# Summing the last four rows of an output projection in two PSUM banks

## The chip, the core and the metric

The kernel runs on one core of a Trainium2 chip. The metric is the device time of one execution in microseconds (us), as the median of several runs. A profile of one execution is read beside it. Engines are named as the profile names them: PE (TensorE, matmuls; PEld are its weight loads), DVE (VectorE), ACT (ScalarE), POOL (GpSimd), SP (SyncE). A q behind an engine's name means its queue, which issues transfers (DMA) and waits for semaphores.

## What is computed

One decode step for one token of width 1024: a layer norm, then an attention over the last 4096 positions of a cache (32 query heads, 4 key and value heads of width 128) with its output projection `wo`, and in parallel an MLP; both are added to the input.

```
xn = layernorm(x)
q  = (xn @ wq) as 32 heads of 128;  k, v = last 4096 rows of each cache, 8 heads share one
o  = softmax(q k^T / sqrt(128)) v
A  = o.reshape(1, 4096) @ wo
B  = gelu(layernorm(xn) @ w1 + b1) @ w2 + b2
out = x + A + B                       # 1 x 1024, bf16
```

Weights and caches are bf16, some 40 MB in all, each read once.

## The kernel before

The kernel streams weights and caches through a ring of four large buffers in SBUF, filled by transfers on the SP queue in a fixed order: keys, `wq`, `w1`, values, `w2`, `wo`. A transfer into a buffer waits for the last reader of what was there. Everything else follows the arrival of the data.

Products of one row vector with a weight matrix are done as matmuls with one column of stationary weights (`lhsT`, 128 x 1) and 512 columns of the matrix streaming past. Each gives one row of 512 sums. To use more of the PE array, the results of two halves of a row (or four quarters) are put at partitions 0, 32 and so on, by `tile_position`.

The part that the change touches is the last one. The final sum of 1024 columns is kept in one PSUM bank, the tile `accf` (128 x 512 fp32): partition 0 holds columns 0 to 511, partition 32 columns 512 to 1023. It starts from `x + b2` (line 178). Then a loop over `chunk_src` (line 337) adds 28 chunks of `w2`, each weighted by a column of `hT` (the MLP's hidden values), and 32 chunks of `wo`, each weighted by a column of `o8` (the attention output, copied from the PSUM tile `o8_ps` at line 332). A chunk is 128 x 1024, that is one row of 1024 for each partition; the text calls a chunk of `wo` a row of it. Each takes two matmuls, one a half (line 341), with `start=False`, so that they add up in `accf`.

The second 16 rows of `wo` arrive in five transfers of 8, 4, 2, 1 and 1 rows, each with a semaphore of its own, so that PE can start on what is there. The very last row is cut into columns 0 to 319 and 320 to 511 (`N1 = 320`), so four matmuls. At the end DVE copies 320 columns of `accf` to the bf16 tile `res` (line 345) and ACT the other 192 (line 346). Two transfers, one on the SP queue and one on the ACT queue, write the two halves of the result (lines 348 and 349).

PSUM tiles that live shortly come from the pool `ps_f`, two banks that are used in turn: `sp`, `mT_ps`, `mc_ps`, `rs_ps`, `o_all` and `o8_ps` among them. Waits between engines are put in by the framework from which tile each operation reads and writes; two engines that read one PSUM tile are put in order. The order of instructions on each engine is that of the program text.

Of the kernel before, what the change touches and what calls it, by code (L numbers as in the profile page):

```python
# [8 lines left out]
FP32 = mybir.dt.float32  # L9
BF16 = mybir.dt.bfloat16  # L10
ACT = mybir.ActivationFunctionType
ALU = mybir.AluOpType
# [4 lines left out]
def kernel(  # L17
# [14 lines left out]
    nc = tc.nc  # L32
    P = 128
# [20 lines left out]
    consts = ctx.enter_context(tc.tile_pool(name="consts", bufs=1))  # L54
# [4 lines left out]
    ps_f = ctx.enter_context(tc.tile_pool(name="ps_f", bufs=2, space=bass.MemoryType.PSUM))  # L59
# [3 lines left out]
    def ring_tile(name):  # L63
        return ring.tile([P, RING_ELEMS], BF16, tag="ring", name=name, align_bytes=256)
# [13 lines left out]
    for i in range(2):  # L78
        t = ring_tile(f"wq{i}")
# [8 lines left out]
    ident_f = consts.tile([P, P], FP32)  # L88
# [83 lines left out]
    accf = ps_acc.tile([P, 512], FP32, tag="accf")  # L172
# [3 lines left out]
    for half in range(2):  # L176
        pr = 32 * half
        nc.tensor.matmul(accf[pr:pr + 1, :], lhsT=ones_bf[0:2, 0:1], rhs=xb2[:, 512 * half:512 * half + 512],
                         start=True, stop=False, tile_position=(0, pr))
# [24 lines left out]
    for i in range(2):  # L204
        t = ring_tile(f"w1{i}")
# [9 lines left out]
    chunk_src = []  # L215
    w2_v = B_w2.rearrange("(p c) n -> p c n", p=P)
    for i in range(2):
        nr = CW2 // 2
        t = ring_tile(f"w2{i}")
# [4 lines left out]
    for i, cuts in enumerate([[0, 16], [0, 8, 12, 14, 15, 16]]):  # L224
        nr = CWO // 2
        t = ring_tile(f"wo{i}")
# [6 lines left out]
    for i, w3 in enumerate(wq_tiles):  # L233
        for r in range(4):
            c = 4 * i + r
            for j in range(NJQ):
                b, t = divmod(j, 4)
                nc.tensor.matmul(accq[32 * t:32 * t + 1, b, :], lhsT=xnT[:, c:c + 1], rhs=w3[:, r, j * 512:(j + 1) * 512],  # L238
                                 start=(c == 0), stop=(c == C - 1), tile_position=(0, 32 * t))
# [8 lines left out]
    for j in range(8):  # L248
        t, b = divmod(j, 2)
        nc.tensor.matmul(acch[32 * t:32 * t + 1, b, :NH], lhsT=ones_bf[0:1, 0:1], rhs=b1_row[:, j * NH:(j + 1) * NH],  # L250
                         start=True, stop=False, tile_position=(0, 32 * t))
    for i, w3 in enumerate(w1_tiles):
        for r in range(4):
            c = 4 * i + r
            for b in range(2):
                for t in range(4):
                    j = 2 * t + b
                    nc.tensor.matmul(acch[32 * t:32 * t + 1, b, :NH], lhsT=yT[:, c:c + 1], rhs=w3[:, r, j * NH:(j + 1) * NH],  # L258
                                     start=False, stop=(c == C - 1), tile_position=(0, 32 * t))
# [3 lines left out]
    for g in range(Hkv):  # L263
        b, th = divmod(g, 2)
# [6 lines left out]
    for a in range(WQ4 // 512):  # L271
        sp = ps_f.tile([P, 512], FP32, tag="pf", name="sp")
        for R in range(4):
            for g in range(Hkv):
                c0 = WQ4 * R + 512 * a
                nc.tensor.matmul(sp[32 * R:32 * R + 32, :], lhsT=qm[:, g, :], rhs=kT[:, g, c0:c0 + 512],  # L276
                                 start=(g == 0), stop=(g == Hkv - 1), tile_position=(0, 32 * R))
# [41 lines left out]
    for c in range(NCH):  # L319
        nc.tensor.matmul(o_all[:].rearrange("h g d -> h (g d)"), lhsT=eTb[:, 32 * c:32 * c + 32], rhs=v4[:, :, c, :],  # L320
                         start=(c == 0), stop=(c == NCH - 1))
# [12 lines left out]

    vec = {"h": lambda c: hT[:, c, 0:1], "o": lambda c: o8[:, c:c + 1]}
    N1 = 320
    for idx, (kind, c, wap) in enumerate(chunk_src):
        last = idx == len(chunk_src) - 1
        for n0, n1 in ((0, N1), (N1, 512)) if last else ((0, 512),):
            for half in range(2):  # L340
                nc.tensor.matmul(accf[32 * half:32 * half + 1, n0:n1], lhsT=vec[kind](c),  # L341
                                 rhs=wap[:, half * 512 + n0:half * 512 + n1],
                                 start=False, stop=last and n0 > 0, tile_position=(0, 32 * half))
    res = consts.tile([33, 512], BF16)
    nc.vector.tensor_copy(out=res[:, 0:N1], in_=accf[0:33, 0:N1])  # L345
    nc.scalar.copy(out=res[:, N1:512], in_=accf[0:33, N1:512])  # L346
    out_v = out.rearrange("a b (t n) -> (a b t) n", t=2)
    nc.sync.dma_start(out=out_v[0:1, :], in_=res[0:1, :])
    nc.scalar.dma_start(out=out_v[1:2, :], in_=res[32:33, :])
# [30 lines left out]
```

## Time and profile before

| | us |
|---|---|
| median of 3 runs | 102.22 (102.12 to 102.40) |
| the profiled execution | 102.17 |
| its span, first to last instruction | 100.4 |
| busy in it: PE / DVE / ACT | 49.5 / 48.8 / 33.8 |
| transfers | 39.92 MB, mean 398 GB/s |

The profile lists, for each group of equal instructions, source line, engine, operation, output and inputs with their shapes, count, busy time, mean duration in ns, and the idle time of the engine just ahead of them with what ended it. The chain of waits follows the last instruction back through whatever released it. A granted clock (PEclk) of 1.00 is full speed of PE. Durations of matmuls are modelled from their starts, so the records of neighbours overlap. Of the span, 1.8 us are missing to the execution's own time; they lie outside.

```profile
PE   0165200009400930194865718997390980299970
DMA  2999999999999998999999998999999999999910
```

These two rows of the page are the busy tenths of PE and of the transfers in 40 slices of the span: the transfers are busy from the first slice almost to the last, and PE works in bursts.

### The profile page before, as it was taken

What the parts mean: (1) busy time and instruction counts of PE and PEld (TensorE: products, weight loads), DVE (VectorE), ACT (ScalarE), POOL (GpSimd) and SP (SyncE); (2) the same over time, 40 slices, a digit from 0 to 9 for tenths busy, and PEclk for the clock granted to TensorE, in tenths of its full rate; (3) what the DMA queues carried; (4) which work ended last, traced back from release to release, by engine and by line L of the source; (5) the groups of instructions that cost most, each with busy time, mean ns of one, the idle gap of its engine ahead of it and who ended that gap; (6) DMA issues with size and microseconds to landing.
All of it is one profiled execution on the core that took longest, in us unless ns stands there. A gap on an engine that the chain in (4) does not pass through costs nothing.

```text
span 100.4 us, 944 instructions
## 1 busy us (share of the span) xinstructions
PE 49.5 (49%) x355; PEld 19.5 (19%) x355; DVE 48.8 (49%) x89; ACT 33.8 (34%) x36; POOL 3.8 (4%) x16
## 2 busy tenths in 40 slices
PE   0165200009400930194865718997390980299970
PEld 0131200003100300022522203343130320033310
DVE  5445499999999999995136061502600000000010
ACT  5000004999999999942020148000000000000001
POOL 6006200000000000000000000000000000000000
PEclk9999999999999999999998555599999669556997
DMA  2999999999999998999999998999999999999910
GB/s 29 396 438 424 558 431 444 418 418 418 418 418 403 514 384 369 491 411 400 393 434 428 424 506 377 498 400 423 457 411 415 431 457 405 418 418 408 380 42 1
DMA packets 2878, 39.92 MB, mean 398 GB/s; under 512 B 309, under 2 KB 311, under 8 KB 698
## 3 DMA queue, kind: packets, MB, share of 16 engines
q1 hardware_dynamic: 2866, 39.85, 93.3%
q8 instruction: 3, 0.05, 0.2%
q10 hardware_dynamic: 8, 0.01, 0.0%
q14 instruction: 1, 0.01, 0.0%
HBM read 39.86 MB, written 0.00 MB: 397 GB/s over the span
## 4 chain that ended last, share of the span: by engine, by line
DMA 80%; PE 13%; SPq 2%; issue 1%; DVE 0%; ACT 0%
DMA wq<-in_A_wq_dram 27%; DMA wo<-in_A_wo_dram 25%; DMA v_sb<-in_A_v_cache_dram 23%; PE o_all L320 9%; DMA k_sb<-in_A_k_cache_dram 5%; PE accq L238 4%; SPq L229 2%; SPq L213 1%; DVE res L345 0%; PE accf L341 0%; ACT res L346 0%
## 5 line engine op out<-in xcount | busy, mean ns | idle before, releaser
L200 ACT COPY kT<-kt_scr 32x1024 bf16<-32x1024 bf16 x26 | 27.1, 1042 | 14.5 <-DVE kt_scr L186 14.2
L186 DVE STREAM_TRANSPOSE kt_scr<-k_sb 128x4096 bf16<-128x4096 bf16 x4 | 17.4, 4412 | 0.0
L202 DVE COPY kT<-kt_scr 32x1024 bf16<-32x1024 bf16 x38 | 15.9, 419 | 0.5
L238 PE MATMUL accq<-wq,xnT 128*1 128x512 bf16 x64 | 7.2, 626 | 18.2 <-DMA wq<-in_A_wq_dram 18.2
L345 DVE CAST res<-accf 33x320 bf16<-33x320 f32 x1 | 0.5, 483 | 25.2 <-PE accf L341 25.2
L341 PE MATMUL accf<-wo,o 128*1 128x512 bf16 (+2 forms) x66 | 9.9, 460 | 5.0 <-DMA wo<-in_A_wo_dram 5.0
L346 ACT CAST res<-accf 33x192 bf16<-33x192 f32 x1 | 0.3, 313 | 35.5 <-DVE res L345 35.5
L320 PE MATMUL o_all<-v_sb,eTb 128*32 128x512 bf16 x32 | 9.2, 459 | 1.6 <-DMA v_sb<-in_A_v_cache_dram 1.6
L341 PE MATMUL accf<-w,hT 128*1 128x512 bf16 x56 | 8.1, 452 | 2.5 <-DMA w<-in_B_w_dram 2.5
L258 PE MATMUL acch<-w,yT 128*1 128x448 bf16 x64 | 5.7, 525 | 6.2 <-DMA w<-in_B_w_dram 6.2
L238 PEld LDWEIGHTS <-xnT 128*1 128x1 bf16 x64 | 2.1, 116 | 22.5 <-issue 22.5
L341 PEld LDWEIGHTS <-o 128*1 128x1 bf16 x66 | 3.3, 98 | 11.9 <-issue 9.8
L320 PEld LDWEIGHTS <-eTb 128*32 128x32 bf16 x32 | 3.5, 113 | 6.9 <-issue 3.0
L341 PEld LDWEIGHTS <-hT 128*1 128x1 bf16 x56 | 2.7, 96 | 7.2 <-issue 5.0
L258 PEld LDWEIGHTS <-yT 128*1 128x1 bf16 x64 | 1.9, 107 | 9.5 <-issue 9.0
L276 PE MATMUL sp<-kT,qm 128*32 128x512 bf16 x32 | 3.4, 588 | 0.4 <-DVE qm L267 0.4
L323 DVE TENSOR_TENSOR o_m<-o_all,grs 32x512 f32<-32x512 f32 x1 | 0.7, 679 | 5.6 <-PE o_all L320 5.6
L123 PE MATMUL x_ps<-ones_bf,xb 1*128 1x1 bf16 x8 | 0.6, 198 | 4.7 <-DMA xb<-in_A_x_dram 4.7
L315 DVE STREAM_TRANSPOSE hT<-h_sb 128x896 bf16<-128x896 bf16 x1 | 1.7, 1704 | 2.4 <-ACT h_sb L313 2.4
L298 ACT ACTIVATE e<-sc,nmx 128x1024 bf16<-128x1024 f32 x1 | 1.1, 1147 | 4.9 <-DVE nmx L295 4.9
L276 PEld LDWEIGHTS <-qm 128*32 128x32 bf16 x32 | 2.1, 133 | 1.4 <-issue 0.9
L281 ACT COPY sc<-sp 128x512 f32<-128x512 f32 x1 | 0.6, 586 | 4.5 <-PE sp L276 4.5
(81 smaller groups left out, 32.0 us busy)
## 6 DMA issues: line engine op xcount, KB each, us to landing
w<-in_B_w_dram SPq DMA_DIRECT2D x4, 3584.0 KB
wq<-in_A_wq_dram SPq DMA_DIRECT2D x2, 4096.0 KB, 26.7
k_sb<-in_A_k_cache_dram SPq DMA_DIRECT2D x4, 1024.0 KB, 6.8
wo<-in_A_wo_dram SPq DMA_DIRECT2D x1, 4096.0 KB, 30.7
v_sb<-in_A_v_cache_dram SPq DMA_DIRECT2D x1, 2048.0 KB, 19.5
v_sb<-in_A_v_cache_dram SPq DMA_DIRECT2D x2, 1024.0 KB, 23.4
wo<-in_A_wo_dram SPq DMA_DIRECT2D x1, 2048.0 KB
wo<-in_A_wo_dram SPq DMA_DIRECT2D x1, 1024.0 KB
```

Source lines behind the costliest of these rows:

```text
L186: nc.vector.transpose(out=scr[:, g, :], in_=k2[:, g, :])
L200: nc.scalar.copy(out=dst, in_=src)
L202: nc.vector.tensor_copy(out=dst, in_=src)
L213: nc.sync.dma_start(out=v4[:, g0:g1, :, :], in_=src)
L229: nc.sync.dma_start(out=tv[:, a:b, :], in_=wo_v[:, nr * i + a:nr * i + b, :])
L238: nc.tensor.matmul(accq[32 * t:32 * t + 1, b, :], lhsT=xnT[:, c:c + 1], rhs=w3[:, r, j * 512:(j + 1) * 512], start=(c == 0), stop=(c == C ...
L258: nc.tensor.matmul(acch[32 * t:32 * t + 1, b, :NH], lhsT=yT[:, c:c + 1], rhs=w3[:, r, j * NH:(j + 1) * NH], start=False, stop=(c == C - 1) ...
L276: nc.tensor.matmul(sp[32 * R:32 * R + 32, :], lhsT=qm[:, g, :], rhs=kT[:, g, c0:c0 + 512], start=(g == 0), stop=(g == Hkv - 1), tile_posit ...
L298: nc.scalar.activation(out=e128[:], in_=sc[:], func=ACT.Exp, bias=nmx[:], scale=scale, accum_out=l_loc[:])
L315: nc.vector.transpose(out=hT[:], in_=h_sb[:].rearrange("p (d c) -> p c d", c=CW2))
L320: nc.tensor.matmul(o_all[:].rearrange("h g d -> h (g d)"), lhsT=eTb[:, 32 * c:32 * c + 32], rhs=v4[:, :, c, :], start=(c == 0), stop=(c == ...
L341: nc.tensor.matmul(accf[32 * half:32 * half + 1, n0:n1], lhsT=vec[kind](c), rhs=wap[:, half * 512 + n0:half * 512 + n1], start=False, stop ...
```

## The change

The last four rows of `wo` no longer go into `accf`. The loop over the first 56 chunks is as before (both halves, 512 columns) and closes `accf`. ACT then copies columns 320 to 511 of it to an fp32 tile in SBUF (`bulk1`) and DVE columns 0 to 319 (`bulk0`). Two new PSUM tiles of the pool `ps_f`, `acct0` (320 columns) and `acct1` (192 columns), are zeroed by DVE in the 33 partitions that are read later. The last four rows are summed into them, each row cut at 320 as only the last was before. Ahead of the third of the four, two fp32 matmuls with columns of the identity `ident_f` add `bulk1` to `acct1`, one a half. At the end DVE adds `acct0` and `bulk0` into `res`, and ACT copies `acct1` into `res`.

In the program's order of instructions, the first memset stands on DVE ahead of the copy of `o8` and the second behind it; the fp32 matmuls wait for ACT's copy of the bulk; DVE's copy of the bulk waits for ACT's; the two output transfers wait for DVE and ACT both. The weight loads ahead of the fp32 matmuls are part of these instructions. Nothing changes on the SP queue ahead of the output.

```diff
-    for idx, (kind, c, wap) in enumerate(chunk_src):
-        last = idx == len(chunk_src) - 1
-        for n0, n1 in ((0, N1), (N1, 512)) if last else ((0, 512),):
+    TAIL = 4
+    n_bulk = len(chunk_src) - TAIL
+    for idx, (kind, c, wap) in enumerate(chunk_src[:n_bulk]):
+        for half in range(2):
+            nc.tensor.matmul(accf[32 * half:32 * half + 1, :], lhsT=vec[kind](c), rhs=wap[:, half * 512:(half + 1) * 512],
+                             start=False, stop=(idx == n_bulk - 1), tile_position=(0, 32 * half))
+    cols = ((0, N1), (N1, 512))
+    bulk = [consts.tile([33, b - a], FP32, name=f"bulk{i}") for i, (a, b) in enumerate(cols)]
+    nc.scalar.copy(out=bulk[1][:], in_=accf[0:33, N1:512])
+    nc.vector.tensor_copy(out=bulk[0][:], in_=accf[0:33, 0:N1])
+    acct = [ps_f.tile([P, b - a], FP32, tag="pf", name=f"acct{i}") for i, (a, b) in enumerate(cols)]
+    for t in acct:
+        nc.vector.memset(t[0:33, :], 0.0)
+    for idx, (kind, c, wap) in enumerate(chunk_src[n_bulk:]):
+        if idx == TAIL - 2:
             for half in range(2):
-                nc.tensor.matmul(accf[32 * half:32 * half + 1, n0:n1], lhsT=vec[kind](c),
+                nc.tensor.matmul(acct[1][32 * half:32 * half + 1, :], lhsT=ident_f[0:33, 32 * half:32 * half + 1], rhs=bulk[1][:],
+                                 start=False, stop=False, tile_position=(0, 32 * half))
+        for t, (n0, n1) in zip(acct, cols):
+            for half in range(2):
+                nc.tensor.matmul(t[32 * half:32 * half + 1, :], lhsT=vec[kind](c),
                                  rhs=wap[:, half * 512 + n0:half * 512 + n1],
-                                 start=False, stop=last and n0 > 0, tile_position=(0, 32 * half))
+                                 start=(idx == 0), stop=(idx == TAIL - 1), tile_position=(0, 32 * half))
     res = consts.tile([33, 512], BF16)
-    nc.vector.tensor_copy(out=res[:, 0:N1], in_=accf[0:33, 0:N1])
-    nc.scalar.copy(out=res[:, N1:512], in_=accf[0:33, N1:512])
+    nc.vector.tensor_tensor(out=res[:, 0:N1], in0=acct[0][0:33, :], in1=bulk[0][:], op=ALU.add)
+    nc.scalar.copy(out=res[:, N1:512], in_=acct[1][0:33, :])
```

In the changed kernel the fp32 matmuls are at line 353, the matmuls of the last four rows at 357, DVE's sum at 361 and ACT's copy at 362.

## The prediction

> **What bounds the kernel now.** I read the chain of waits first, because only what lies on its last link can move the time, then the timeline of the last microseconds, then the groups for the price of each operation.
>
> The page says that the span is one long transfer; the chain in order of time shows how the last transfer turns into the end.
>
> ```profile
> span 100.4 us, 944 instructions
> DMA 80%; PE 13%; SPq 2%; issue 1%; DVE 0%; ACT 0%
> ...
> 71.55 25.41 DMA wo<-in_A_wo_dram
> 96.96 0.04 issue
> 97.00 0.40 PE accf L341 x4
> 97.40 0.02 issue
> 97.42 0.49 DVE res L345
> 97.92 0.02 issue
> 97.94 0.31 ACT res L346
> ```
>
> The transfers carry 80% of the chain, and the change touches none of them. What it can touch is the stretch behind the landing of the last `wo` row at 96.96: the matmuls of that row, then DVE's copy of 320 columns, then ACT's copy of 192, one after the other, then the two output transfers. The timeline of that stretch has each step's start and length, and in brackets what its engine waited for:
>
> ```profile
> 95.52 1.25 PE L341 MATMUL accf<-wo,o 128*1 128x512 bf16 x8
> 95.79 0.30 PEld L341 LDWEIGHTS <-o 128*1 128x1 bf16 x4 [0.18 <-issue]
> 96.39 0.08 PEld L341 LDWEIGHTS <-o 128*1 128x1 bf16 x2 [0.30 <-issue]
> 97.00 0.38 PE L341 MATMUL accf<-wo,o 128*1 128x320 bf16 x4 [0.23 <-DMA wo<-in_A_wo_dram]
> 97.42 0.48 DVE L345 CAST res<-accf 33x320 bf16<-33x320 f32 x1 [25.17 <-PE accf L341]
> 97.94 0.31 ACT L346 CAST res<-accf 33x192 bf16<-33x192 f32 x1 [35.49 <-DVE res L345]
> 98.28 0.32 SPq L348 DMA_DIRECT2D out_dram<-res  x1
> ```
>
> I number the last 16 rows of `wo` 0 to 15. The eight matmuls from 95.52 are rows 11 to 14, two halves each; the weight loads at 95.79 and 96.39 mark where rows 12 and 14 began, with idle time ahead of them, so PE is waiting for data there and no longer working off a backlog. Row 15 starts at 97.00. ACT's copy waits for DVE's, not for PE: that serial 0.31 us is what the change goes after. From row 15's start to the output transfer is 98.28 - 97.00 = 1.28 us.
>
> **The change part by part.** *The finish.* Row 15 now goes into two PSUM tiles, and DVE and ACT each read one. In the changed program ACT's last copy waits for PE and for the second memset, not for DVE's sum, so the two run side by side. DVE no longer waits for the 192-column pair either. The prices:
>
> ```profile
> L341 PE MATMUL accf<-wo,o 128*1 128x320 bf16 x2 | 0.3, 296 | 0.2 <-DMA wo<-in_A_wo_dram 0.2
> L341 PE MATMUL accf<-wo,o 128*1 128x192 bf16 x2 | 0.2, 244 | 0.0
> L323 DVE TENSOR_TENSOR o_m<-o_all,grs 32x512 f32<-32x512 f32 x1 | 0.7, 679 | 5.6 <-PE o_all L320 5.6
> L241 DVE CAST q_sb<-accq 128x512 bf16<-128x512 f32 x1 | 0.7, 692 | 0.0
> L320 PEldq EVENT_SEMAPHORE  x1: 51/51/51, 60.4 to 60.4; - x1
> ```
>
> At 512 columns a two-input DVE operation out of PSUM (679 ns) costs what a copy does (692), so I price the new sum of 320 columns like the old copy, 0.48 us. Let T be the start of row 15. DVE starts at T + 0.30 (its pair) + 0.04 (the step from 97.38, the last matmul's end, to 97.42), and ends at T + 0.82. ACT starts 0.08 us later than DVE (the 52 ns by which 320 and 192 columns differ say 0.41 ns a column, so a 192-column pair streams for 0.08) and needs 0.31: it ends at T + 0.73, earlier. The transfers were issued 0.03 us after the last copy (97.94 + 0.31 to 98.28). Now they wait for two engines; the second wait is a semaphore instruction of its own, for which I take 0.05 us (the 51 ns row; the lower bound is nothing). The issue comes at T + 0.82 + 0.03 + 0.05 = T + 0.90 in place of T + 1.28. **Gain if T stays at 97.00: 0.38 us.**
>
> *The bulk copies and the fp32 matmuls.* These lie in front of rows 14 and 15 on PE, so they decide T. Row 11's second half is the last of the bulk. It starts at 95.52 and lasts 0.38:
>
> ```profile
> L341 PE MATMUL accf<-wo,o x66: 243/379/634, 87.3 to 97.1; 128*1 128x512 bf16 x62, 128*1 128x320 bf16 x2, 128*1 128x192 bf16 x2
> L242 ACT CAST q_sb<-accq 128x512 bf16<-128x512 f32 x1 | 0.6, 587 | 2.8 <-DVE q_sb L241 2.8
> L281 ACT COPY sc<-sp 128x512 f32<-128x512 f32 x1 | 0.6, 586 | 4.5 <-PE sp L276 4.5
> ```
>
> An fp32 result costs ACT no more than a bf16 one (586 against 587), so its copy of 192 columns is 0.31: 95.90 + 0.04 + 0.31 = 96.25, and with the step to PE 96.30. Meanwhile PE works off rows 12 and 13, which take 0.22 us each whether cut at 320 or not, from 95.79 to 96.22; it then waits 0.08 us for ACT. Nothing but rows 14 and 15 is queued behind that wait, and behind them the two finishing operations and the output transfers. DVE's copy of the bulk runs after ACT's, 96.29 to 96.77, and is covered by DVE's own wait until T + 0.34.
>
> An fp32 matmul of this shape is not in the trace. The nearest rows:
>
> ```profile
> L286 PE MATMUL mT_ps<-ident_f,m_loc 128*1 128x128 f32 x1 | 0.3, 269 | 2.1 <-DVE m_loc L284 2.1
> L302 PE MATMUL rs_ps<-l_loc,sel x2: 193/203/213, 58.6 to 58.7; 128*32 128x1 f32 x2
> 53.77 0.27 PE L286 MATMUL mT_ps<-ident_f,m_loc 128*1 128x128 f32 x1 [2.07 <-DVE m_loc L284]
> 53.98 0.36 PE L258 MATMUL acch<-w,yT 128*1 128x448 bf16 x4
> ```
>
> In bf16 a matmul lasts 165 ns plus 0.41 ns a column (296 and 244). The fp32 one of 128 columns lasts 269, so 104 for its columns: 0.81 ns each, twice bf16. One fp32 product is recorded as two passes (`rs_ps`, x2 for one call), so 192 columns cost 2 x 0.156 = 0.31 us a half. The two halves lie in different column strips of the array. If they overlap as the bf16 halves do, both take 0.31; if the second can start only with the first one's second pass, 0.47; if they queue, 0.62; if every pass ran to the end of its record (4 x (0.165 + 0.156)), 1.28. The `rs_ps` passes began within 0.1 us of each other with records of 0.2, which speaks against the last; I take **0.47**. Coming back to full rows costs something too: from `mT_ps` to the next matmul are 0.21 us, 0.10 more than its columns. So F = 0.47 + 0.10 = 0.57, with ends of 0.31 and 1.28.
>
> Here a rule speaks against the change. The changed program gives the fp32 matmuls a tile of 64 rows between tiles of 128.
>
> ```profile
> 71.78 0.25 PE L330 MATMUL o_ps<-o_bf,spread 32*128 32x32 bf16 x4 [2.06 <-DVE o_bf L327]
> 71.96 0.30 PEld L341 LDWEIGHTS <-hT 128*1 128x1 bf16 x6
> 71.96 0.59 PE L341 MATMUL accf<-w,hT 128*1 128x512 bf16 x4
> 72.07 0.19 DVE L332 CAST o<-o_ps 128x32 bf16<-128x32 f32 x1 [0.34 <-PE o_ps L330]
> ```
>
> Going from 32 rows (L330) to 128 (L341), the next matmul began at 71.96, before the last record of L330 ended at 72.03, so no wait for the whole record is seen. A wait for the whole record would cost 0.165 a switch and not 0.10. The Trainium skill, "TensorEngine Tiling (Array Packing)", section Key Properties, says that changing the tiling mode drains TensorE, while changing the tile alone does not. By it as a full drain, F would be 0.64 and the gain 0.22. The row shows a shorter price than that.
>
> Then T = 96.30 + F + 0.22 (row 14) = 97.09 against 97.00: row 14's data, used at 96.39 before, is there long before PE asks for it. **T slips by 0.09, and 0.38 - 0.09 = 0.29 us remain.** F is free up to 0.48; the gain is gone at F = 0.86.
>
> *The rest.* The two memsets and DVE's place in the queue:
>
> ```profile
> L173 DVE MEMSET accf<- 128x512 f32 x1 | 0.5, 485 | 0.1
> L175 DVE MEMSET accq<- 128x1024 f32 x1 | 0.9, 912 | 0.2 <-issue 0.2
> ```
>
> 0.83 ns a column and 60 ns: the first memset, of 320 columns, takes about 0.33 us and stands ahead of DVE's copy of `o8`, in the 0.34 us in which DVE waited for `o_ps` (the row at 72.07). Without that cover it would delay `o8` by as much, whose first use is at 87.3, 15 us later. The second, of 192, about 0.22, stands behind. The SP and ACT queues keep their order, and no transfer of inputs waits for anything new. Splitting rows 12 to 14 adds six matmuls, but the same columns.
>
> The sum against the profiled execution: 102.17 us, of which 100.4 are span and 1.8 lie outside. 102.17 - 0.29 = 101.88; against the median of the runs, 102.22, it is **101.93**.
>
> **The rivals.** (B) *The halves overlap fully.* F is 0.31 + 0.10 = 0.41, below 0.48, T stays, and the gain is 0.38: 101.84. For it: the eight matmuls of 0.38 us within 1.25 us, so the bf16 halves share their time. Against: two passes of one half have to queue on its strip. (C) *The halves queue, or the switches drain.* F 0.64 to 0.72, gain 0.14 to 0.22: 102.04. (D) *Slower: each fp32 pass runs to the end of its record.* F = 1.28 + 0.10, T = 97.90, 0.90 late: 0.38 - 0.90 = 0.52 slower, 102.74. It decides from F = 0.86, and is slower by 0.3% from 1.17; only the close starts of the `rs_ps` passes speak against it, and those had one column. (E) *Slower: PE is behind when the tail starts.* The clock came back to full just in time:
>
> ```profile
> 88.00:92.00 4.00, 4.00 (x22) 1.26 (x20) 0.00 (x0) 0.00 (x0) 0.00 (x0) 0.50 0.97 414
> 92.00:92.50 0.50, 0.50 (x8) 0.13 (x6) 0.00 (x0) 0.00 (x0) 0.00 (x0) 0.79 1.05 442
> 92.50:97.00 4.50, 4.26 (x38) 1.52 (x35) 0.00 (x0) 0.00 (x0) 0.00 (x0) 1.00 0.67 264
> ```
>
> At 0.50 PE does half as much, so each microsecond that the full clock comes later puts row 11 back by half. The kernel before has 0.55 us of waiting left ahead of row 15 (three rows of 0.22 from 95.79 end at 96.45); the changed one has none, so it would pay all of it: with 1.5 us, 0.75 - 0.29 = 0.46 slower, 102.68. The gain is gone at 0.6 us. The three runs before lie within 0.28 us. (F) *It does not do what it says*: the last copies still run in turn, and the time is 102.2.
>
> **How the numbers follow.** About 0.3% (0.31 us) is what a measurement of this kernel can tell from no change. My case A (F near 0.57, gain about 0.29, so across the bound as a few hundredths of F decide) 0.38; B 0.27; C 0.10; D 0.12; E 0.10; F 0.03. Faster by over 0.3%: half of A and nearly all of B, 0.46. Within: half of A, C, F and a fifth of E, 0.34. Slower: D and the rest of E, 0.20. The time is that of A, 101.93. The range goes down to B less the 0.1 us by which the runs spread, 101.70, and up beyond C into E, 102.40, which leaves out D and half of E.
>
> **What would show it.** Right: in the changed trace two fp32 records a half at L353, the first near 96.3; ACT's L362 and DVE's L361 overlapping; DVE starting 0.34 us after row 15; the output issued 0.90 us after it. Wrong: an idle time of PE ahead of row 15 that ends with the landing (B), or fp32 records that take over 0.75 us together (C, D); PE still busy with row 11 after 95.9 (E); L362 beginning only when L361 ends (F).

## The result and the profile after

Over ten runs of each, the changed kernel takes 101.94 us (101.75 to 102.12) and the kernel before 102.30 (101.96 to 102.42): a ratio of 0.9969, with a 95% interval of 0.9956 to 0.9982. It is faster, by 0.32 us with an interval of 0.18 to 0.45, so the bound of 0.3% (0.31 us) that the prediction set lies inside the interval. Two later groups of runs gave 0.9951 (0.9939 to 0.9964) and 0.9970 (0.9960 to 0.9981).

The profiled execution took 101.75 us, of which 100.0 are span. Its timeline, to be laid beside that of before:

```profile
94.56 1.03 PE L341 MATMUL accf<-wo,o 128*1 128x512 bf16 x8
95.63 0.31 ACT L345 COPY bulk<-accf 33x192 f32<-33x192 f32 x1 [31.86 <-PE accf L341]
95.79 0.60 PE L357 MATMUL acct<-wo,o 128*1 128x320 bf16 x8 [0.20 <-DMA wo<-in_A_wo_dram]
95.97 0.48 DVE L346 COPY bulk<-accf 33x320 f32<-33x320 f32 x1 [21.87 <-ACT bulk L345]
96.32 0.49 PE L353 MATMUL acct<-bulk,ident_f 33*1 33x192 f32 x4
96.74 0.69 PE L357 MATMUL acct<-wo,o 128*1 128x320 bf16 x8
97.04 0.09 PEld L357 LDWEIGHTS <-o 128*1 128x1 bf16 x3
97.38 0.48 DVE L361 TENSOR_TENSOR res<-acct,bulk 33x320 bf16<-33x320 f32 x1 [0.93 <-PE acct L357]
97.46 0.31 ACT L362 CAST res<-acct 33x192 bf16<-33x192 f32 x1 [1.52 <-PE acct L357]
97.93 0.31 SPq L364 DMA_DIRECT2D out_dram<-res  x1
```

DVE's sum and ACT's copy now overlap, and both wait for PE. The fp32 matmuls start at 96.32, row 14 at 96.74 and row 15 with the weight load at 97.04, 0.04 us after its data landed at 97.00. From there to the output are 0.89 us; before they were 1.28. In this execution row 15 did not slip behind its data.

### The profile page after: what moved, and what is told of

It is laid out like the page before. It is cut to its first block, busy times and chain, and to the rows that moved or that the text cites. A ratio compares the mean times of both kernels' runs of the same rounds, so it can differ in the third digit from the quotient of the medians.

```text
span 100.0 us, 970 instructions
## 1 busy us (share of the span) xinstructions
PE 51.2 (51%) x365; PEld 20.0 (20%) x365; DVE 49.7 (50%) x92; ACT 34.1 (34%) x37; POOL 3.8 (4%) x16
## 3 DMA queue, kind: packets, MB, share of 16 engines
q1 hardware_dynamic: 2866, 39.85, 93.6%
## 4 chain that ended last, share of the span: by engine, by line
DVE 38%; DMA 24%; PE 21%; issue 9%; POOL 3%; ACT 2%; SPq 1%; POOLq 1%; ACTq 0%
DMA wo<-in_A_wo_dram 24%; DVE kt_scr L186 17%; DVE kT L202 16%; PE o_all L320 10%; PE sp L276 4%; PE acch L258 3%; ACT e L298 1%; DVE eTb L300 1%; PE qT_ps L262 1%; DVE m_loc L284 1%; PE acct L357 1%; SPq L229 1%; DVE q_sb L241 1%; POOLq L391 1%; POOL spread L110 1%
## 5 line engine op out<-in xcount | busy, mean ns | idle before, releaser
L346 DVE COPY bulk<-accf 33x320 f32<-33x320 f32 x1 | 0.5, 483 | 21.9 <-ACT bulk L345 21.9
L341 PE MATMUL accf<-wo,o 128*1 128x512 bf16 x56 | 8.3, 459 | 6.0 <-DMA wo<-in_A_wo_dram 5.9
L320 PE MATMUL o_all<-v_sb,eTb 128*32 128x512 bf16 x32 | 10.0, 491 | 1.0 <-DVE zcol L311 1.0
L258 PE MATMUL acch<-w,yT 128*1 128x448 bf16 x64 | 6.3, 572 | 6.0 <-DMA w<-in_B_w_dram 6.0
L341 PEld LDWEIGHTS <-o 128*1 128x1 bf16 x56 | 2.8, 97 | 11.4 <-issue 9.2
```

Source lines behind the costliest of these rows:

```text
L341: nc.tensor.matmul(accf[32 * half:32 * half + 1, :], lhsT=vec[kind](c), rhs=wap[:, half * 512:(half + 1) * 512], start=False, stop=(idx == ...
```

## The experiments

All ratios are to the kernel before, on the same chip, with 95% intervals. T is the start of row 15.

**The changed kernel again (e1).**

> The changed kernel as it is, as the reference for the others of this group. Theory 1 (the finishing copies run side by side, and the fp32 matmuls fit into the wait for the last row): 0.30 to 0.40 us below the kernel before; row 15 starts within 0.05 us of its landing. Theory 2 (as in the prediction: the fp32 matmuls put row 15 back by about 0.09 us): 0.29 us below, and row 15 starts 0.1 us or more after its landing.

101.74 us, 0.9951 (0.9939 to 0.9964): 0.40 us below 102.14. In its trace row 15 followed its landing (97.02) by the same 0.04. Theory 1 holds for this execution.

**One bank for the last four rows (e2).**

```diff
-    acct = [ps_f.tile([P, b - a], FP32, tag="pf", name=f"acct{i}") for i, (a, b) in enumerate(cols)]
-    for t in acct:
-        nc.vector.memset(t[0:33, :], 0.0)
+    acct_one = ps_f.tile([P, 512], FP32, tag="pf", name="acct_one")
+    nc.vector.memset(acct_one[0:33, :], 0.0)
+    acct = [acct_one[:, a:b] for a, b in cols]
...
-        for t, (n0, n1) in zip(acct, cols):
+        for t, (n0, n1) in zip(acct, cols) if idx else ((acct_one, (0, 512)),):
...
```

> As the changed kernel, but the last four rows go into one PSUM tile of 512 columns (one memset of 512 columns; row 12 is not cut at 320). Bulk copies and fp32 matmuls stay. Theory 1 and 2: the gain comes from the two copies running side by side, so all of it goes: ACT's copy starts only when DVE's sum ends, the output is issued 1.28 us after row 15 starts in place of 0.89, and the time is that of the kernel before, within 0.1 us. Rival (the gain is in the shorter way of the last four rows through PE, or in the earlier start of DVE): at least 0.1 us of it stays.

102.23 us, 1.0008 (0.9996 to 1.0020). The whole gain is gone. In its timeline ACT waits for DVE again:

```profile
97.32 0.60 PE L357 MATMUL acct_one<-wo,o 128*1 128x320 bf16 x8
97.96 0.48 DVE L361 TENSOR_TENSOR res<-acct_one,bulk 33x320 bf16<-33x320 f32 x1 [0.60 <-PE acct_one L357]
98.48 0.31 ACT L362 CAST res<-acct_one 33x192 bf16<-33x192 f32 x1 [1.63 <-DVE res L361]
98.82 0.31 SPq L364 DMA_DIRECT2D out_dram<-res  x1
```

From T (97.54) to the output are 1.28 us, as expected. So the gain needs the second bank, and the way of the last rows through PE brings nothing by itself. The second bank does two things, and this run takes away both: ACT's copy runs beside DVE's, and DVE starts without waiting for the 192-column pair, 0.34 us after T and not 0.42. By the timelines the earlier start is 0.08 of the 0.39 us, and the rest is ACT's copy, which is off the path; no run separates the two. This profiled execution (102.72, the longest of the kernel's twelve) shows something else too. PE ran from row 14 into row 15 without a pause, and row 15 started at 97.54, 0.44 us after its landing at 97.10. The full clock had come late:

```profile
88.00:93.00 5.00, 5.00 (x26) 1.54 (x24) 0.00 (x0) 0.00 (x0) 0.00 (x0) 0.50 0.96 410
93.00:93.50 0.50, 0.50 (x6) 0.11 (x4) 0.00 (x0) 0.00 (x0) 0.00 (x0) 0.72 1.01 418
```

That is rival E of the prediction, here in a variant of the changed kernel: the bulk closed late (ACT's copy started at 96.53 and not at 95.63), and copy and fp32 matmuls ran behind it.

**The fp32 pair twice (e3).**

```diff
+    zero_b = consts.tile([33, 512 - N1], FP32, name="zero_b")
+    nc.gpsimd.memset(zero_b[:], 0.0)
...
+            for more in range(1):
+                for half in range(2):
+                    nc.tensor.matmul(acct[1][32 * half:32 * half + 1, :], lhsT=ident_f[0:33, 32 * half:32 * half + 1], rhs=zero_b[:],
+                                     start=False, stop=False, tile_position=(0, 32 * half))
```

> As the changed kernel, with the fp32 pair followed by a second pair that adds a tile of zeros. Theory 1, by the changed kernel's trace (two passes 0.16 us apart, halves side by side, 0.25 us from the last pass to row 14): the pair costs 0.32 us more, PE is ready for row 15 at 97.27 and not 96.95, so row 15 slips 0.23 us behind a landing at 97.00, and the time rises by 0.23 us over the changed kernel. Theory 2 (halves staggered, 0.47 a pair, nothing hidden): 0.47 us more. Rival (the fp32 matmuls are not on the path at all): no change.

102.11 us, 0.9994 (0.9984 to 1.0005): the gain is gone here as well. The trace shows the size that theory 1 gave:

```profile
96.27 0.49 PE L355 MATMUL acct<-bulk,ident_f 33*1 33x192 f32 x4
96.60 0.49 PE L359 MATMUL acct<-zero_b,ident_f 33*1 33x192 f32 x4
97.02 0.60 PE L363 MATMUL acct<-wo,o 128*1 128x320 bf16 x8
97.58 0.48 DVE L367 TENSOR_TENSOR res<-acct,bulk 33x320 bf16<-33x320 f32 x1 [1.16 <-PE acct L363]
98.13 0.31 SPq L370 DMA_DIRECT2D out_dram<-res  x1
```

The second pair begins 0.33 us after the first, and row 14 starts 0.75 after the first pair began (0.42 with one pair). T is 97.23, 0.26 after the landing at 96.97 in place of 0.04. So 0.10 of the added 0.33 was free, and the rest put row 15 back. The median rose by more than these 0.22, by 0.37 over e1; where the rest comes from in the other executions was not traced.

**Two banks for all rows (e4).**

```diff
-    for idx, (kind, c, wap) in enumerate(chunk_src):
-        last = idx == len(chunk_src) - 1
-        for n0, n1 in ((0, N1), (N1, 512)) if last else ((0, 512),):
+    fin = ((accf[:, 0:N1], 0, N1), (accq[:, 0, 0:512 - N1], N1, 512))
...
+    for idx, (kind, c, wap) in enumerate(chunk_src):
+        for t, n0, n1 in fin:
...
```

> The kernel before, but all rows of w2 and wo are cut at 320 columns and summed in two PSUM banks (the second is a bank of accq, zeroed again after q is copied out, with x and b2 put in by a matmul of its own); DVE and ACT each copy one bank at the end. No bulk copies, no fp32 matmuls, no sum on DVE. PE has 120 matmuls more, with the same columns. Theory 1: the same finish and the same row 15, so the time of the changed kernel within 0.1 us. Theory 2: the 0.09 us that the fp32 matmuls cost are saved too, 0.1 us below the changed kernel. Rival (a weight load for each of twice as many matmuls makes PE late at half clock): slower than the changed kernel by 0.1 us or more, with PE still at work when row 15 lands.

101.88 us, 0.9967 (0.9954 to 0.9980). Without bulk copies and fp32 matmuls the gain is about that of the changed kernel, within what the intervals can tell. The finish is the same, and PE is idle ahead of row 15:

```profile
97.19 0.30 PE L345 MATMUL accf<-wo,o 128*1 128x320 bf16 x2 [0.27 <-DMA wo<-in_A_wo_dram]
97.54 0.48 DVE L349 CAST res<-accf 33x320 bf16<-33x320 f32 x1 [25.01 <-PE accf L345]
97.62 0.31 ACT L350 CAST res<-accq 33x192 bf16<-33x192 f32 x1 [35.22 <-PE accq L345]
98.08 0.31 SPq L352 DMA_DIRECT2D out_dram<-res  x1
```

This is 0.89 us from T, as in the changed kernel; but the row itself landed at 97.15 and not at 97.00. That fits the median, which is 0.14 above that of e1, though the two intervals overlap. Why the row landed later is the matter of e12.

**0.85 us of PE work more ahead of `wo` (e5 in the changed kernel, e6 in the one before).**

```diff
+        if idx == CW2:
+            for extra in range(2):
+                for half in range(2):
+                    nc.tensor.matmul(accq[32 * half:32 * half + 1, 1, :], lhsT=vec[kind](c), rhs=wap[:, half * 512:(half + 1) * 512],
+                                     start=True, stop=True, tile_position=(0, 32 * half))
```

> The changed kernel with four matmuls of 512 columns more at the first row of wo, whose sums go to a PSUM bank that nobody reads: at half clock some 0.85 us of PE work. Theory (the changed kernel has no slack on PE ahead of row 15, since copies and fp32 matmuls fill it): of the 0.85 the idle times ahead of rows 8 and 12 take up 0.4 at most, so row 15 slips by 0.4 to 0.85 and the time rises by 0.5 us over the changed kernel, above the kernel before. Rival (the last row's landing sets the time in both, PE has room): the time stays within 0.1 us of the changed kernel.

> The kernel before with the same four matmuls more. Theory: here 0.55 us of waiting is left ahead of row 15 besides the idle times, so row 15 still starts with its landing in most executions: 0 to 0.2 us over the kernel before. Rival (0.85 us of PE work cost the same anywhere in this stretch): 0.4 us or more.

e5: 101.84 us (101.62 to 102.66), 0.9978 (0.9960 to 0.9997). The median did not rise by 0.5 over the changed kernel, so the expectation fell in its size. What changed is the spread: three of the twelve runs took 102.19, 102.34 and 102.66, where none of the 22 runs of the changed kernel took more than 102.12. No run of the changed kernel stands beside e5 on its chip, though, and there the runs of the kernel before spread more as well: up to 0.39 above their median, against 0.25 and 0.18 on the chips of e1 and e10. So not all of e5's 0.82 need come from the added work. In the profiled execution row 15 did slip, but its data had come early:

```profile
96.46 0.49 PE L358 MATMUL acct<-bulk,ident_f 33*1 33x192 f32 x4
96.88 0.60 PE L362 MATMUL acct<-wo,o 128*1 128x320 bf16 x8
97.44 0.48 DVE L366 TENSOR_TENSOR res<-acct,bulk 33x320 bf16<-33x320 f32 x1 [0.52 <-PE acct L362]
```

DVE starts 0.34 after T, so T is 97.10, and the landing was at 96.79. e6: 102.20 us (101.89 to 102.52), 0.9999 (0.9986 to 1.0011), as expected: in the median the kernel before swallows the same work. Its profiled execution, at 102.36, did not: the full clock came at 93.1, and row 15 started at 97.25, 0.23 after its landing at 97.02. I had taken the profiled clock as typical. It came to full at 92.2 in the profile of before, and between 90.7 and 93.4 in those of the changed kernel and of e1 to e11. Where it comes 1.5 us earlier, PE has half of that, 0.75 us, more room (an estimate from the clock of 0.50).

**The output cut by columns (e7).**

```diff
-    nc.sync.dma_start(out=out_v[0:1, :], in_=res[0:1, :])
-    nc.scalar.dma_start(out=out_v[1:2, :], in_=res[32:33, :])
+    nc.sync.dma_start(out=out_v[:, 0:N1], in_=res[0:33:32, 0:N1])
+    nc.scalar.dma_start(out=out_v[:, N1:512], in_=res[0:33:32, N1:512])
```

> The changed kernel with the output cut by columns and not by halves: SP's transfer takes the 320 columns of both halves that DVE writes, ACT's the 192 that ACT writes, so each waits for one engine. Theory (the second wait costs 0.05 us, and DVE's sum is the later of the two): SP issues 0.03 us after DVE's sum in place of 0.06, the time falls by 0.03 to 0.05 us, if two pieces of 640 bytes take no longer than one of 1024. Rival: two pieces in each transfer take longer to land, and the time does not fall or rises by up to 0.1 us.

102.37 us, 1.0020 (1.0008 to 1.0033): 0.4 to 0.6 us above the medians of the changed kernel in its three groups, far beyond what the rival gave.

```profile
97.29 0.48 DVE L361 TENSOR_TENSOR res<-acct,bulk 33x320 bf16<-33x320 f32 x1 [0.60 <-PE acct L357]
97.71 0.57 ACTq L365 DMA_DIRECT2D out_dram<-res  x1
97.80 0.61 SPq L364 DMA_DIRECT2D out_dram<-res  x1
```

The wait got shorter as expected: SP issues 0.03 us after DVE's sum (97.29 + 0.48 to 97.80) and not 0.07. But issuing two pieces takes 0.61 us in place of 0.31, and the transfer lands 1.87 us after its issue (99.67) in place of 1.27 (97.93 to 99.20).

**Two banks for all rows, cut at 288 (e8).** The kernel of e4 with `N1 = 288`.

> The kernel with two banks for all rows, cut at 288 in place of 320 columns. DVE's copy costs 483 ns at 320 and 692 at 512 columns, so 448 at 288; ACT's 313 at 192 and 587 at 512, so 340 at 224; DVE also starts 0.01 us sooner. Theory: both copies end within 0.02 us of each other, the output is issued 0.05 us sooner after row 15 than with 320 (0.84 and not 0.89), and the time is 0.05 us below that of two banks cut at 320: 0.40 us below the kernel before if row 15 starts with its landing. Rival (the end is not set by DVE's copy): no change against 320.

101.87 us, 0.9978 (0.9962 to 0.9994). From T (97.20) to the output (98.04) are 0.84 us, as worked out. In the time this does not show against e4.

**A tail of eight rows, cut at 288 (e9, with e10 beside it and e11 with the added work).**

```diff
-    N1 = 320
-    TAIL = 4
+    N1 = 288
+    TAIL = 8
...
-        if idx == TAIL - 2:
+        if idx == TAIL - 4:
```

> The changed kernel with eight rows in the two banks in place of four, cut at 288 and not 320 columns, and the fp32 matmuls ahead of the fifth of the eight (row 12), where PE waits for data anyway. Theory: with the cut at 288 the output is issued 0.84 us after row 15 starts and not 0.89; and the fp32 matmuls no longer stand right ahead of rows 14 and 15, so that about 0.45 us of waiting is left ahead of row 15 as in the kernel before. Row 15 starts with its landing in nearly all executions: the time is 0.05 to 0.15 us below the changed kernel. Rival (row 15 starts with its landing in the changed kernel too, in nearly all executions): 0.05 us below it at most, not to be told from it.

> The changed kernel once more, beside e9 and e11 on the same chip: 0.30 to 0.40 us below the kernel before.

> The kernel of e9 with the four matmuls more at the first row of wo (0.85 us of PE work at half clock), as in e5. Theory (0.45 us of room ahead of row 15): the median stays within 0.1 us of e9, and the highest of its executions lies less above the median than in e5, where it was 0.8 us. Rival (its room is used up as well): the spread is that of e5.

e9: 101.69 us (101.58 to 101.98), 0.9967 (0.9954 to 0.9979); e10: 101.80 (101.67 to 101.94), 0.9970 (0.9960 to 0.9981). They are not to be told apart. e11: 101.87 (101.61 to 102.14), 0.9972 (0.9960 to 0.9983). Its median lies 0.18 above that of e9, where 0.1 at most was expected, though by the intervals the two are not to be told apart. Its highest run lies 0.27 above its median, that of e5 0.82 above; as e5 ran on a chip with a wider spread, this does not show that the room is what made the difference. In the trace of e9 PE waits again:

```profile
95.50 0.54 PE L353 MATMUL acct<-bulk,ident_f 33*1 33x224 f32 x4
95.97 0.82 PE L357 MATMUL acct<-wo,o 128*1 128x288 bf16 x12
97.02 0.38 PE L357 MATMUL acct<-wo,o 128*1 128x288 bf16 x4 [0.23 <-DMA wo<-in_A_wo_dram]
97.86 0.31 SPq L364 DMA_DIRECT2D out_dram<-res  x1
```

0.84 us from T again, and some idle time of PE ahead of T. By the timelines this variant is worth 0.05 us where row 15 is not late, and more only in the executions where it is; seven runs do not resolve that.

**Few matmuls (e12).** Only the loops are thinned out; all transfers stay.

> The kernel before with most matmuls left out (kept: one of eight rows of wq and of w1, one head group of the scores, two of the 32 of the values, none of w2, seven rows of wo), all transfers kept: 73 matmuls and not 355, so that PE never comes to the point of its program (some 180 matmuls and weight loads) at which the instruction transfers at 37 and 64 us occur. Theory (the last two of the sixteen landings of a transfer, 0.8 to 1.4 us behind the middle one, are engines that carried 16 KB of PE's instructions): no such transfers, no landing over 0.6 us behind the middle one, the last row lands near 96.2 and not 97.0, and the time falls by 0.6 to 1.2 us. Rival (two of the engines are slower for another cause): the landings are spread as before, the last one 1.2 to 1.4 us behind the middle one.

One execution, at 101.51 us, 0.61 below the kernel before on that chip. (Six rows of `wo` were kept, not seven; the profile counts 81 matmul records in place of 355.) Two rows of the transfers by queue (packets, MB, share of the engines' time), of the kernel before:

```profile
q1 hardware_dynamic: 2866, 39.85, 93.3%
q8 instruction: 3, 0.05, 0.2%
```

and of e12:

```profile
q1 hardware_dynamic: 2866, 39.85, 93.8%
q10 hardware_dynamic: 8, 0.01, 0.0%
```

The same 2866 packets of data, and no packet on the queue q8, whose three packets of 16 KB start at 37, 64 and 96 us in the kernel before. They keep step with PE's instructions: PE had started 177, 413 and 696 matmuls and weight loads by then, and in e4 177, 421 and 695. In e12 it started 162 in all. The last half microseconds of the transfers in the kernel before (the last two numbers are the transfers' busy share and GB/s):

```profile
95.50:96.00 0.50, 0.50 (x7) 0.17 (x4) 0.00 (x0) 0.00 (x0) 0.00 (x0) 1.00 0.30 102
96.00:96.50 0.50, 0.49 (x6) 0.17 (x3) 0.00 (x0) 0.00 (x0) 0.00 (x0) 1.00 0.13 49
96.50:97.00 0.50, 0.27 (x2) 0.00 (x0) 0.00 (x0) 0.00 (x0) 0.00 (x0) 1.00 0.02 8
```

and in e12:

```profile
95.50:96.00 0.50, 0.46 (x2) 0.08 (x2) 0.00 (x0) 0.00 (x0) 0.00 (x0) 1.00 0.04 16
96.00:96.50 0.50, 0.45 (x6) 0.09 (x3) 0.00 (x0) 0.00 (x0) 0.00 (x0) 1.00 0.00 0
```

Each of these transfers has sixteen landings, as many as the core has DMA engines. Of those of the last row, the middle ones come at 95.65 before and at 95.54 in e12. The last two come at 96.78 and 96.96 before, and at 95.85 and 96.14 in e12. So the expectation held: without instruction transfers no landing of the last row is more than 0.6 us behind the middle one, and the time is lower by 0.61, at the lower end of what was expected. Not all of the 0.82 us between the two last landings shows in the time, because the matmuls of row 15 took longer in e12 (DVE starts 0.63 us after T, and not 0.42).

The landings of the earlier transfers bear it out in time. In the kernel before, the last landing is 0.19 us behind the middle one in the transfer that lands at 32 us, and 1.41 behind at 41; at 68 two landings are late, by 1.31 and 1.57. In e12 the last one is 0.84 behind at 41, so a part of the first step is there without the packet at 37, and the second last stays within 0.42. The trace does not name an engine, so that the two late ones carried the packets at 37 and 64 us is inferred, and e12 left out other work too. In e4 and e8, which have 120 matmuls and as many weight loads more, the third such transfer comes at 83 us, inside the stream. Two landings of e4 are over a microsecond late in the transfer that lands at 76 us and three in the next one, at 86; the last row's last landing comes at 97.15 and 97.16. That fits, but no run changed only this.

## Why the prediction was right, point by point

- *The finish.* 0.90 us from T to the output was forecast, 0.89 measured; DVE's sum 483 ns (0.48 forecast), its start 0.34 after T (0.34), the step from its end to the output 0.07 (0.08). e2 shows that the gain hangs on this step: without the second bank it is gone.
- *The start of the fp32 matmuls.* Forecast 96.30, measured 96.32, but not for the reason given. ACT's copy ended at 95.94 and not at 96.25, because PE was at full speed earlier (91.1 and not 92.2), so PE did not wait for it. Rows 12 and 13 streamed until 96.22, as forecast, and 0.10 us more passed before the first fp32 matmul began. The prediction put this way into the fp32 matmuls at nothing; it is the same 0.53 us from row 12 to the first fp32 matmul in e1 and e3. That the sum came out is luck.
- *F.* This is the term that was mis-sized: 0.57 forecast, 0.42 measured (96.32 to 96.74). The pass was right (0.16 us for 192 fp32 columns, by e3 0.33 for a pair of two), and so was the way back, 0.09 for 0.10. The row behind that 0.10 does not show it, though: `mT_ps` is itself a matmul of 128 rows, so nothing returns to full rows there, and that its step came out alike is luck. What was wrong is the stagger. Four records of 320 ns fit into 0.49 us, so the two halves overlap fully, and a pair costs 0.32 and not 0.47. That is rival B, to which I gave 0.27.
- *The slip of T.* Forecast 0.09, measured none in the three profiled executions of the changed kernel (T 0.04 to 0.05 after the landing; 0.04 before). PE would have been ready at 96.95, 0.09 ahead; in e3 the second pair used up this room and put T back by the rest.
- *The number.* B's gain of 0.38 is near the 0.36 between the two medians, and A's 0.29 is inside the interval as well. That the forecast of 101.93 met 101.94 so closely is luck: the 0.29 holds a slip of 0.09 that did not come, and it was taken from a median of three runs (102.22), where ten runs of the kernel before gave 0.08 us more (102.30).
- *Rival D* is excluded by the records of L353, rival *F* by the overlap of L361 and L362. *Rival C*'s drain: row 14 starts at 96.74, before the last fp32 record ends at 96.81. The Trainium skill, "TensorEngine Tiling (Array Packing)", section Key Properties, has a change of tiling mode drain TensorE; here the change of rows from 64 to 128, with that from fp32 to bf16, cost 0.09 us beyond the columns, and the change the other way 0.10, less than the record's remaining 0.165, so a full drain as I priced it is not seen.
- *Rival E* was seen in one execution of e2 (T 0.44 late), not in the changed kernel itself: its 22 runs reach 102.12 at most, and E was priced at 102.68. A clock that came to full 1.1 us later than in the kernel before put row 11 back by 0.59 us there (96.11 against 95.52), about the half that the prediction took. In e5 the added work went with some longer executions, with the doubt about the chip said above.

## What to carry to other kernels

Where two engines finish a result in turn, look whether the order is a need or only that both read one PSUM tile: a second bank here turned 0.48 + 0.31 us into 0.48, and how the sums came into two banks (fp32 matmuls, or all rows cut) made no difference that could be measured (0.9951 and 0.9967, with overlapping intervals). Work that is put into a wait is free only up to the wait: one fp32 pair fitted with 0.09 us to spare, a second one cost the whole gain. Judge such a tail by several profiles, since the clock's phase moves the wait from execution to execution.

## What the runs showed that was not expected

- Two fp32 matmuls at partitions 0 and 32, of two passes each, run side by side: 0.32 us for the pair of 192 columns.
- An output transfer in two pieces of 640 bytes took 0.30 us more to issue and 0.60 more from issue to landing than one of 1024 bytes. It undid more than the two banks had gained.
- PE's own program is fetched in 16 KB transfers beside the data, and in their presence two of sixteen landings come over a microsecond late at the end. Without them (e12, one execution, most matmuls left out) the last row landed 0.8 us sooner and the time was 0.6 us lower, more than this change brought. Fewer PE instructions, or a fetch that falls behind the stream, might be the larger gain; no version that computes the whole result with so few instructions was tried.
